# Attention and GeGLU block: runs of five overlapping tokens on even and odd partitions, another load order on two queues, and batches 1 and 2 prepared inside blocks 0 and 1

## Chip, cores and metric

One core of one Trainium2 chip runs the whole program. The metric is the device time of one execution in microseconds (us), smaller is better. The kernel before was timed in 3 runs; the median stands for it.

## What is computed

The inputs are q, k and v (8 batches, 8 heads, 576 tokens, 64 features, float32) and three weights. Attention without a token-by-token matrix comes first, then a gated feed-forward over all 4608 tokens:

```python
q_s = softmax(q, axis=-1)            # over the 64 features
k_s = softmax(k, axis=2)             # over the 576 tokens
kv  = einsum('bhsd,bhse->bhde', k_s, v)
att = einsum('bhsd,bhde->bhse', q_s, kv)
x   = att.transpose(0, 2, 1, 3).reshape(4608, 512)
out = (gelu(x @ w_gate) * (x @ w_val)) @ w_out      # 512 -> 1536 -> 512
```

## The kernel before

The order of the work on every engine is the order of the program text: nothing is rescheduled. Eight batches are eight blocks of 512 tokens; the last 64 tokens of each batch (its remainder) are gathered in `xtr`, and all eight remainders make a ninth block of 512 tokens.

**Attention of a batch** has these steps. `exp_main` and `exp_rem` (L127 to L139) turn q and k into `eq` and `ek` on ACT, by Exp. `cast_v_main` and `cast_v_rem` copy v to float16 on POOL. `norm_sum` and `norm_mul` (L156 to L171) divide `eq` by its sums per token and head on DVE, four heads at a time. `unit_kv` (L175) multiplies `ek` and v for two pairs of heads on PE (10 matmuls) and scales the product into `kv_sb` on DVE. `unit_t` (L198) transposes `eq` on PE and copies it to `eqt` on DVE; `unit_trem` does it for the remainder. `unit_x` (L223) multiplies `kv_sb` and `eqt` into `psx`, and a copy puts it in `xt`, the input of the block; `unit_xrem` fills `xtr`.

**A block** is twelve steps `ffn_fi` (L241): four matmuls into `psg` and four into `psv`, then Gelu on ACT (`gl`) and a product on DVE (`ht`). Below, FI 3 is the fourth of these steps. `ffn_out` (L259) then takes four slices of 128 tokens (NS 0 to 3), 12 matmuls each, into `psy`; DVE copies each to `yo`, and stores go out. `psg`, `psv` and `psy` share six PSUM buffers, the pieces of attention two others.

**Order.** All loads are on the queue of SP: k, v, q of batch 0 in two halves of heads, then weights, then batch 1. A DMA for 512 tokens puts four consecutive tokens on each of 128 partitions (packets of 1 KB); a second one puts the 64 tokens of the remainder on 64 partitions (packets of 256 B). Attention of batch 0 stands ahead of block 0. That of batch 1 stands behind the twelve steps of block 0, between and after its slices NS 1 to 3, and likewise batch 2 in block 1. From block 2 on, the attention of the next batch rides inside the twelve steps (`attention_units`, `norm_units`), and the Exp of the batch after that stands behind them.

Of the kernel before, what the change touches and what calls it, by code (L numbers as in the profile page):

```python
# [18 lines left out]
def kernel(  # L19
# [392 lines left out]
```

## Time and profile before

| | us |
|---|---|
| median of 3 runs | 353.28 (353.16 to 353.89) |
| profiled execution | 353.71 |
| its span, first to last instruction | 351.8 |
| PE busy | 319.6 (91%) |
| DVE, ACT, POOL busy | 179.9, 135.7, 42.4 |
| mean DMA rate | 135 GB/s |

A profile row names the line, the engine, the operation, the tile written and the tiles read, and the shape. Matmul rows overlap, so a busy PE is not a PE at its peak rate; what counts is when a matmul follows which.

### The profile page before, as it was taken

Reading aid. Unit: us, or ns where it says so; the run is one execution under the profiler, and the core shown is the slowest. Engines: PE = TensorE matmul, PEld = TensorE weight load, DVE = VectorE, ACT = ScalarE, POOL = GpSimd, SP = SyncE. Lnnn points to the kernel's source line nnn. Section 1 sums busy time; section 2 is a strip of 40 time slices with the busy share of each in tenths; the row PEclk is TensorE's granted clock in tenths of the full one; section 3 lists DMA queues with packets and bytes.
Section 4 is the critical chain, followed back from the end, with each engine's and each line's share of the span. In section 5 each row is a group of like instructions: output and inputs, shape, how many; then the busy total and the mean of one; then the engine's idle time right before and its main releaser. Section 6 shows DMA issues by size and latency. Waiting matters only on the chain.

```text
span 351.8 us, 4287 instructions
## 1 busy us (share of the span) xinstructions
PE 319.6 (91%) x1680; PEld 152.8 (43%) x1680; DVE 179.9 (51%) x283; ACT 135.7 (39%) x184; POOL 42.4 (12%) x36
## 2 busy tenths in 40 slices
PE   0259999499987999999999999999999999999994
PEld 0234445244443544454444444544544444444441
DVE  2582337934386963396339524953494334334331
ACT  3403363043762247424743483248325123203310
POOL 2376620402000200002000200020000000000000
PEclk9999999789996999999999999999999999999999
DMA  7999999893016900296039404940300020011013
GB/s 192 330 388 386 344 278 284 241 269 94 3 60 188 270 6 2 96 276 153 0 117 287 120 2 135 277 112 0 121 1 0 8 113 0 2 60 60 2 30 89
DMA packets 45395, 47.45 MB, mean 135 GB/s; under 512 B 13632, under 2 KB 38208, under 8 KB 45376
## 3 DMA queue, kind: packets, MB, share of 16 engines
q1 hardware_dynamic: 45376, 47.19, 46.3%
q8 instruction: 13, 0.21, 0.3%
q14 instruction: 6, 0.05, 0.1%
HBM read 37.75 MB, written 9.44 MB: 134 GB/s over the span
## 4 chain that ended last, share of the span: by engine, by line
PE 85%; DVE 10%; DMA 2%; issue 1%; SPq 1%; ACT 0%
PE psg L244 27%; PE psv L248 27%; PE psy L262 24%; DVE eq L169 3%; DVE rq L159 2%; PE psx L226 2%; DMA qt<-in_q_dram 2%; PE pst L205 2%; PE pskv L180 2%; DVE xt L229 1%; DVE yo L267 1%; DVE eqt L208 1%; DVE kv_sb L188 1%; PE pstr L214 1%; DVE rrq L163 0%
## 5 line engine op out<-in xcount | busy, mean ns | idle before, releaser
L253 DVE SCALAR_TENSOR_TENSOR ht<-psv,gl 128x512 f16<-128x512 f32 x108 | 74.1, 686 | 92.1 <-PE psv L248 91.5
L251 ACT ACTIVATE gl<-psg 128x512 f32<-128x512 f32 x108 | 64.5, 597 | 144.7 <-PE psg L244 136.1
L244 PE MATMUL psg<-xt,wg_sb 128*128 128x512 f16 x384 | 101.8, 389 | 0.0
L248 PE MATMUL psv<-xt,wv_sb 128*128 128x512 f16 x384 | 99.5, 382 | 0.0
L262 PE MATMUL psy<-wo_sb,ht 128*128 128x512 f16 x432 | 95.0, 379 | 0.0
L248 PEld LDWEIGHTS <-wv_sb 128*128 128x128 f16 x432 | 42.6, 99 | 52.5 <-issue 2.7
L262 PEld LDWEIGHTS <-ht 128*128 128x128 f16 x432 | 41.8, 98 | 49.4
L244 PEld LDWEIGHTS <-wg_sb 128*128 128x128 f16 x432 | 41.6, 99 | 46.0 <-issue 2.8
L267 DVE TENSOR_SCALAR yo<-psy 128x512 f32<-128x512 f32 x36 | 24.8, 690 | 60.7 <-PE psy L262 60.7
L147 POOL CAST v<-vt 128x2048 f16<-128x2048 f32 (+1 forms) x9 | 16.4, 1824 | 179.7 <-DMA vt<-in_v_dram 166.6
L159 DVE TENSOR_REDUCE rq<-eq 128x20 f32<-128x1280 f16 x16 | 23.6, 1476 | 9.6 <-ACT eq L136 9.6
L169 DVE TENSOR_TENSOR eq<-eq,rrq 128x1280 f16<-128x1280 f16 x16 | 25.4, 1590 | 0.2
L205 PE MATMUL pst<-ident,eq 128*128 128x128 f16 x128 | 11.5, 242 | 14.5 <-DVE rck L185 7.8
L180 PE MATMUL pskv<-v,ek 128*128 128x130 f16 x160 | 12.6, 231 | 9.9 <-POOL v L147 9.5
L129 ACT ACTIVATE eq<-qt 128x2048 f16<-128x2048 f32 (+1 forms) x9 | 15.4, 1709 | 6.4 <-DMA qt<-in_q_dram 6.4
L205 PEld LDWEIGHTS <-eq 128*128 128x128 f16 x128 | 9.0, 108 | 19.3 <-DVE eq L169 9.3
L180 PEld LDWEIGHTS <-ek 128*128 128x128 f16 x160 | 11.1, 102 | 13.7 <-ACT ek L129 6.0
L129 ACT ACTIVATE ek<-kt 128x2048 f16<-128x2048 f32 (+1 forms) x9 | 15.5, 1719 | 3.6 <-DMA kt<-in_k_dram 3.5
L238 ACT CAST xtr<-psxr 128x256 f16<-128x256 f32 x8 | 3.0, 372 | 34.9 <-PE psxr L236 34.9
L226 PE MATMUL psx<-eqt,kv_sb 128*128 128x512 f16 x32 | 14.0, 463 | 1.9 <-DVE eqt L208 1.1
L231 ACT CAST xt<-psx 128x512 f16<-128x512 f32 x20 | 11.7, 585 | 9.6 <-PE psx L226 9.6
L248 PE MATMUL psv<-xtr,wv_sb 128*128 128x512 f16 x48 | 12.3, 379 | 0.0
(33 smaller groups left out, 121.1 us busy)
## 6 DMA issues: line engine op xcount, KB each, us to landing
out_dram<-yo SPq DMA_DIRECT2D x16, 512.0 KB, 2.6
kt<-in_k_dram SPq DMA_DIRECT2D x7, 1024.0 KB, 7.9
vt<-in_v_dram SPq DMA_DIRECT2D x7, 1024.0 KB, 10.3
qt<-in_q_dram SPq DMA_DIRECT2D x7, 1024.0 KB, 10.3
wgst<-in_moe_w_gate_dram SPq DMA_DIRECT2D x3, 1024.0 KB, 12.3
wvst<-in_moe_w_val_dram SPq DMA_DIRECT2D x3, 1024.0 KB, 13.6
wost<-in_moe_w_out_dram SPq DMA_DIRECT2D x3, 1024.0 KB, 14.6
kt<-in_k_dram SPq DMA_DIRECT2D x2, 512.0 KB, 5.9
```

The source lines that it names most:

```text
L129: nc.scalar.activation(out=dst[:, 0:NM, h0 * D:h1 * D].rearrange("p n (h d) -> p h n d", d=D), in_=tiles[(nm, b)][:, h0:h1, :].rearrange(" ...
L159: nc.vector.reduce_sum(rq, eq_b[b % 2][:, :, h0 * D:h1 * D].rearrange("p n (h d) -> p n h d", d=D), axis=mybir.AxisListType.X)
L169: nc.vector.tensor_tensor(out=e, in0=e, in1=rr[(b, h0)].unsqueeze(-1).to_broadcast((P, NM + 1, n, D)), op=ALU.mult)
L180: nc.tensor.matmul(pskv[:, j, :], ek_b[b % 2][:, n, hp * P:(hp + 1) * P], v16_b[b % 2][:, n, 2 * hp:2 * hp + 2, 0:VW], start=(n == 0), sto ...
L205: nc.tensor.transpose(pst[:, j, n * P:(n + 1) * P], eq_b[b % 2][:, n, hp * P:(hp + 1) * P], ident)
L226: nc.tensor.matmul(psx, st[(b, "kv", hp)].rearrange("p h e -> p (h e)"), st[(b, "eqt")][:, hp, 0:MAIN], start=True, stop=True)
L244: nc.tensor.matmul(psg, wg_sb[:, ci, fi * P:(fi + 1) * P], xt[:, ci, :], start=(ci == 0), stop=(ci == HP - 1))
L248: nc.tensor.matmul(psv, wv_sb[:, ci, fi * P:(fi + 1) * P], xt[:, ci, :], start=(ci == 0), stop=(ci == HP - 1))
L251: nc.scalar.activation(out=gl, in_=psg, func=ACTF.Gelu)
L253: nc.vector.scalar_tensor_tensor(out=ht, in0=psv, scalar=_H_SCALE, in1=gl, op0=ALU.mult, op1=ALU.mult)
L262: nc.tensor.matmul(psy, hts[fi][:, ns * P:(ns + 1) * P], wo_sb[:, fi, :], start=(fi == 0), stop=(fi == NFI - 1))
L267: nc.vector.tensor_scalar(out=yo[:, ns % 2, :], in0=psy, scalar1=1.0 / _H_SCALE, scalar2=None, op0=ALU.mult)
```

## The change

A batch is now seen as 64 runs of nine tokens. Run m lies on partitions 2m and 2m+1: the even one holds its tokens 0 to 4, the odd one its tokens 4 to 8, so token 4 is loaded twice. Position 0 counts on even partitions alone: v there is multiplied by `even` (1 on even partitions, 0 on odd ones), and the column of ones with it. The remainder of a batch is now the first token of each run, position 0, and the separate loads, Exps and casts of remainders are gone. Each load becomes two DMAs, one for the even and one for the odd partitions. For batch 0 one goes to SP's queue and one to ACT's, in the order q, k, v, with position 0 of q left for later (`q0r`, `eq0r`). Weights come in halves of the former pieces, through eight buffers of their own. Before and during batch 0, 22 matmuls whose product nobody reads are issued (`warm_pe`), and tables of ACT are loaded by an Exp and a Gelu on a tile `tiny` (`preload`). The first three steps of block 1 are split by head pairs (`ffn_first`), block 0 takes `psy` in two halves of six matmuls (NS 0 to 3 the first halves, NS 4 to 7 the second), the ninth block stands before the last batch, and the last stores go out on two queues.

```diff
-    def load_main(src, nm, b, h0, h1):
+    def load(src, nm, b, h0, h1, n0, engs):
         key = (nm, b)
         if key not in tiles:
-            tiles[key] = ldp.tile([P, H, NM * D], f32, name=f"{nm}t", tag="ld")
+            tiles[key] = ldp.tile([P, H, NC * D], f32, name=f"{nm}t", tag="ld")
+        for t in range(2):
+            engs[t].dma_start(
+                out=tiles[key][t:P:2, h0:h1, n0 * D:NC * D],
+                in_=src[b, h0:h1].rearrange("h (m n) d -> m h (n d)", n=NT)[
+                    :, :, (4 * t + n0) * D:(4 * t + NC) * D])
...
-    def load_rem(src, nm, b):
-        t = rmp.tile([64, H, D], f32, name=f"{nm}r", tag="rm")
-        nc.sync.dma_start(out=t, in_=src[b, :, MAIN:S, :].rearrange("h p d -> p h d"))
-        tiles[(nm + "r", b)] = t
-    def load_batch(b):
-        for src, nm in ((k, "k"), (v, "v"), (q, "q")):
-            load_main(src, nm, b, 0, H)
-            load_rem(src, nm, b)
...
+    def cast_v(b, h0, h1, eng="pool", parts=(0, 1)):
+        t, d = tiles[("v", b)], v16_b[b % 2]
+        if 1 in parts:
+            copy_on(eng, d[:, 1:NC, h0:h1, 0:D].rearrange("p n h d -> p h n d"),
+                    t[:, h0:h1, D:NC * D].rearrange("p h (n d) -> p h n d", d=D))
+        if 0 in parts:
+            dst, src = d[:, 0, h0:h1, 0:D], t[:, h0:h1, 0:D]
+            if eng == "act":
+                nc.scalar.activation(out=dst, in_=src, func=ACTF.Copy, scale=even[:, 0:1])
+            else:
+                (nc.gpsimd if eng == "pool" else nc.vector).tensor_scalar(
+                    out=dst, in0=src, scalar1=even[:, 0:1], scalar2=None, op0=ALU.mult)
+    def norm(b, hp, eng="dve", n0=0, n1=NC):
+        n = n1 - n0
+        e = eq_b[b % 2][:, n0:n1, hp * P:(hp + 1) * P].rearrange("p n (h d) -> p n h d", d=D)
+        rq = att.tile([P, n, 2], f32, name="rq", tag="rq", bufs=4)
+        nc.vector.reduce_sum(rq, e, axis=mybir.AxisListType.X)
+        rrq = att.tile([P, n, 2], f32, name="rrq", tag="rrq", bufs=4)
         nc.vector.reciprocal(out=rrq, in_=rq)
-        rr[(b, h0)] = rrq
-    def norm_mul(b, h0, h1):
-        n = h1 - h0
-        e = eq_b[b % 2][:, :, h0 * D:h1 * D].rearrange("p n (h d) -> p n h d", d=D)
+        (nc.gpsimd if eng == "pool" else nc.vector).tensor_tensor(
+            out=e, in0=e, in1=rrq.unsqueeze(-1).to_broadcast((P, n, 2, D)), op=ALU.mult)
...
+    def warm_pe(n):
+        ps = ps_big.tile([P, 512], f32, name="pswarm", tag="mm")
+        for _ in range(n):
+            nc.tensor.matmul(ps, ident, warm, start=True, stop=True)
+    def preload(func):
+        nc.scalar.activation(out=tiny, in_=tiny, func=func)
...
+    def ffn_first(xt, after):
+        ps = []
+        for fi in range(len(after)):
+            psg = ps_big.tile([P, 512], f32, name="psg", tag="mm")
+            mm_gv(psg, wg_sb, xt, fi, range(0, 2))
+            psv = ps_big.tile([P, 512], f32, name="psv", tag="mm")
+            mm_gv(psv, wv_sb, xt, fi, range(0, 2))
+            ps.append((psg, psv))
+            for f in after[fi]:
+                f()
+        for fi, (psg, psv) in enumerate(ps):
+            mm_gv(psg, wg_sb, xt, fi, [2])
+            mm_gv(psv, wv_sb, xt, fi, [2])
+        hts = []
+        for fi, (psg, psv) in enumerate(ps):
+            mm_gv(psg, wg_sb, xt, fi, [3])
+            mm_gv(psv, wv_sb, xt, fi, [3])
+            hts.append(gate(psg, psv))
+        return hts
...
+    QA = (nc.sync, nc.scalar)
+    load(q, "q", 0, 0, 4, 1, QA)
+    load(q, "q", 0, 4, 8, 1, QA)
+    load(k, "k", 0, 0, H, 0, QA)
+    load(v, "v", 0, 0, H, 0, QA)
+    for c in range(NW):
         load_w_gv(c)
     for c in range(3):
         load_w_o(c)
+    load(q, "q", 1, 0, H, 0, SY2)
+    for c in range(3, NO):
+        load_w_o(c)
+    for h0 in (0, 4):
+        load(k, "k", 1, h0, h0 + 4, 0, SY2)
+        load(v, "v", 1, h0, h0 + 4, 0, SY2)
+    nc.sync.dma_start(out=q0r, in_=q[0].rearrange("h (m n) d -> m h (n d)", n=NT)[:, :, 0:D])
...
+    preload(ACTF.Exp)
+    exp("q", 0, 0, 4, 1)
+    exp("q", 0, 4, 8, 1)
+    exp("k", 0, 0, 4)
+    exp("k", 0, 4, 8)
+    preload(ACTF.Gelu)
+    warm_pe(16)
+    norm(0, 0, "dve", 1)
+    norm(0, 1, "pool", 1)
+    norm(0, 2, "dve", 1)
+    norm(0, 3, "pool", 1)
+    unit_t(0, 0, "dve")
+    warm_pe(6)
+    cast_v(0, 0, 4, "dve")
+    cast_v(0, 4, 6, "act")
+    cast_v(0, 6, 8, "pool")
+    unit_t(0, 1, "dve")
...
+    cast_w("wg", 0, "pool", 0, 128)
+    unit_x(0, 0, "act", True)
...
+    at(0, FI, NFI - 1, L(exp, "q", 1), L(exp, "k", 1, 0, 4),
+       L(cast_w_o, 3), L(cast_w_o, 4, "dve"), L(norm, 1, 0), L(cast_w_o, 5),
+       L(norm, 1, 1, "pool"), L(norm, 1, 2), L(cast_v, 1, 0, 4),
+       L(norm, 1, 3, "pool"), L(exp, "k", 1, 4, 8), L(cast_v, 1, 4, 6, "act"), L(cast_v, 1, 6, 8),
+       L(preload, ACTF.Gelu))
+    at(0, NS, 5, L(unit_t, 1, 0))
+    at(0, NS, 6, L(unit_kv, 1, 0))
+    at(0, NS, 7, L(unit_x, 1, 0, "act", True), L(unit_x, 1, 1, "dve", True),
+       L(unit_t, 1, 1))
+    first1 = [[L(unit_kv, 1, 1)], [L(unit_x, 1, 2, "act")], [L(unit_x, 1, 3, "dve")]]
...
+    at(1, FI, 4, L(norm, 2, 1))
+    at(1, FI, 5, L(norm, 2, 2))
+    at(1, FI, 6, L(norm, 2, 3))
+    at(1, FI, 7, L(unit_t, 2, 0))
+    at(1, FI, 8, L(exp, "k", 2), L(cast_v, 2, 0, H))
+    at(1, FI, 9, L(unit_t, 2, 1))
+    at(1, FI, 10, L(unit_trem, 2))
+    at(1, FI, 11, L(unit_kv, 2, 0), L(unit_kv, 2, 1), L(load_batch, 3),
+       L(exp, "q", 3), L(exp, "k", 3), L(exp_rem0), L(cast_v, 3, 0, H))
+    at(1, NS, 0, L(unit_x, 2, 0, "dve"), L(unit_x, 2, 1, "dve"))
+    at(1, NS, 1, L(unit_x, 2, 2, "dve"), L(unit_x, 2, 3, "dve"))
+    at(1, NS, 2, L(unit_xrem, 2, "dve"))
+    at(1, NS, 3, L(norm_rem0))
+    at(2, FI, 5, L(unit_trem, 0))
+    at(2, FI, 8, L(unit_xrem, 0))
...
+            for i in range(HP):
+                at(b, FI, i, L(norm, n, i))
+            at(b, FI, 0, L(unit_kv, n, 0))
+            at(b, FI, 2, L(unit_kv, n, 1))
+            at(b, FI, 4, L(unit_t, n, 0))
+            at(b, FI, 6, L(unit_t, n, 1))
+            at(b, FI, 7, L(unit_trem, n))
+            for i in range(HP):
+                at(b, FI, 7 + i, L(unit_x, n, i))
+            at(b, FI, 11, L(unit_xrem, n))
```

The loads at the start, on SP's queue (`kt`, `vt`, `qt` are the tiles of 512 tokens or, now, of five positions; `kr`, `vr`, `qr` the remainders; `wgst` and `wvst` weights before their cast). Before:

```order
L89 DMA kt<-in_k_dram 128x4x256
L95 DMA kr<-in_k_dram 64x8x64
L89 DMA vt<-in_v_dram 128x4x256
L95 DMA vr<-in_v_dram 64x8x64
L89 DMA qt<-in_q_dram 128x4x256
L95 DMA qr<-in_q_dram 64x8x64
L89 DMA kt<-in_k_dram 128x4x256
L89 DMA vt<-in_v_dram 128x4x256
L89 DMA qt<-in_q_dram 128x4x256
L109 DMA wgst<-in_moe_w_gate_dram 128x4x512
```

Now, on the same queue (ACT's queue has the first three rows as well, for the odd partitions):

```order
L104 DMA qt<-in_q_dram 64x4x256 x2
L104 DMA kt<-in_k_dram 64x8x320
L104 DMA vt<-in_v_dram 64x8x320
L115 DMA wgst<-in_moe_w_gate_dram 128x4x256
L115 DMA wvst<-in_moe_w_val_dram 128x4x256
```

q moved from third to first, remainders are gone, and each row fills 64 partitions.

DVE between the last `ht` of block 0 and the first `xt` of batch 1 (`rq` and `rrq` are the sums and their reciprocals, `rck` belongs to `kv_sb`). Before:

```order
L253 SCALAR_TENSOR_TENSOR ht<-psv,gl 128x512 x12
L267 TENSOR_SCALAR yo<-psy 128x512 x2
L185 RECIPROCAL rck<-pskv 128x2
L188 SCALAR_TENSOR_TENSOR kv_sb<-pskv,rck,mask 128x128 x2
...
L159 TENSOR_REDUCE rq<-eq_104 128x20
L163 RECIPROCAL rrq<-rq 128x20
L169 TENSOR_TENSOR eq_104<-eq_104,rrq 128x5x256
L267 TENSOR_SCALAR yo<-psy 128x512
```

Now:

```order
L272 SCALAR_TENSOR_TENSOR ht<-psv,gl 128x512 x12
L125 CAST wo_sb<-wost 128x1024
L165 TENSOR_REDUCE rq<-eq_108 128x10
L167 RECIPROCAL rrq<-rq 128x10
L168 TENSOR_TENSOR eq_108<-eq_108,rrq 128x5x128
...
L340 TENSOR_SCALAR yo<-psy 128x512 x2
L125 COPY eqt<-pst 128x2x512
L340 TENSOR_SCALAR yo<-psy 128x512
L196 RECIPROCAL rck<-pskv 128x2
L199 SCALAR_TENSOR_TENSOR kv_sb<-pskv,rck,mask 128x128 x2
```

All four sums (one per pair of heads) and two of the four products now stand ahead of the first `yo`; the other two products went to POOL.

ACT in block 1, where `gl` is the Gelu. Before:

```order
L251 ACTIVATE gl<-psg 128x512 x12
L129 ACT_TABLE_LOAD
L129 ACTIVATE ek_96<-kt 128x8x4x64
L136 ACTIVATE ek_96<-kr 64x512
L129 ACTIVATE eq_97<-qt 128x8x4x64
L136 ACTIVATE eq_97<-qr 64x512
```

Now:

```order
L270 ACTIVATE gl<-psg 128x512 x4
L143 ACT_TABLE_LOAD
L143 ACTIVATE eq_103<-qt 128x8x5x64
L270 ACT_TABLE_LOAD
L270 ACTIVATE gl<-psg 128x512
L123 CAST xtr<-psxr 128x4x64
...
L143 ACT_TABLE_LOAD
L143 ACTIVATE ek_102<-kt 128x8x5x64
L270 ACT_TABLE_LOAD
```

The two Exps of batch 2 moved from behind the twelve Gelus to places after the fourth and the ninth, each between two table loads.

## Rows read from the trace of the kernel before

**Rows 1.** The page: its head, and PE's busy tenths in 40 slices.

```profile
span 351.8 us, 4287 instructions
...
PE   0259999499987999999999999999999999999994
```

**Rows 2.** Windows: stretch, length, busy us (instructions) of PE, PEld, DVE, ACT, POOL, clock, DMA share, GB/s.

```profile
60.00:80.00 20.00, 15.04 (x75) 6.94 (x73) 13.31 (x17) 4.56 (x7) 4.17 (x3) 0.83 0.97 256
```

**Rows 3.** The chain that ended last: start us, length us, what.

```profile
26.69 1.71 PE psg L244 x4
...
30.11 1.56 PE psg L244 x4
...
35.98 0.86 PE psg L244 x4
...
136.72 10.36 PE psy L262 x48
...
171.18 10.36 PE psy L262 x48
...
336.72 10.37 PE psy L262 x48
```

**Rows 4.** Timeline of the start: start us, length us, engine, line, operation, [idle before <-releaser].

```profile
4.90 1.06 ACT L129 ACTIVATE ek<-kt 128x1024 f16<-128x1024 f32 x1 [2.89 <-DMA kt<-in_k_dram]
...
6.58 0.63 ACT L136 ACTIVATE ek<-kr 64x512 f16<-64x512 f32 x1 [0.62 <-DMA kr<-in_k_dram]
...
13.21 1.06 ACT L129 ACTIVATE ek<-kt 128x1024 f16<-128x1024 f32 x1 [0.63 <-DMA kt<-in_k_dram]
...
16.19 1.06 ACT L129 ACTIVATE eq<-qt 128x1024 f16<-128x1024 f32 x1 [1.93 <-DMA qt<-in_q_dram]
...
19.34 1.24 PE L180 MATMUL pskv<-v,ek 128*128 128x130 f16 x10 [0.45 <-DVE xt L229]
...
26.50 1.90 PE L244 MATMUL psg<-xt,wg_sb 128*128 128x512 f16 x4
```

**Rows 5.** Timeline between blocks 0 and 1.

```profile
62.68 1.89 POOL L147 CAST v<-vt 128x2048 f16<-128x2048 f32 x1 [10.56 <-DMA vt<-in_v_dram]
62.72 3.20 DVE L169 TENSOR_TENSOR eq<-eq,rrq 128x1280 f16<-128x1280 f16 x1
64.52 1.87 POOL L152 CAST v<-vr 64x512 f16<-64x512 f32 x1
...
70.70 1.84 PE L244 MATMUL psg<-xt,wg_sb 128*128 128x512 f16 x4
```

**Rows 6.** Timeline in block 1 and at the start of block 2.

```profile
97.41 1.31 PE L180 MATMUL pskv<-v,ek 128*128 128x130 f16 x20
...
111.60 1.87 PE L244 MATMUL psg<-xt,wg_sb 128*128 128x512 f16 x4
```

**Rows 7.** Lines, shapes apart: engine, operation, count | busy us, mean ns | idle before.

```profile
L169 DVE TENSOR_TENSOR eq<-eq,rrq 128x1280 f16<-128x1280 f16 x16 | 25.4, 1590 | 0.2
L159 DVE TENSOR_REDUCE rq<-eq 128x20 f32<-128x1280 f16 x16 | 23.6, 1476 | 9.6 <-ACT eq L136 9.6
L129 ACT ACTIVATE eq<-qt 128x2048 f16<-128x2048 f32 x7 | 13.3, 1895 | 0.6 <-DMA qt<-in_q_dram 0.6
L208 DVE COPY eqt<-pst 128x1024 f16<-128x1024 f16 x16 | 10.8, 682 | 0.9 <-PE pst L205 0.9
L188 DVE SCALAR_TENSOR_TENSOR kv_sb<-pskv,rck,mask 128x128 f16<-128x128 f32 x32 | 9.7, 346 | 0.6
L129 ACT ACT_TABLE_LOAD x7 | 9.0, 1283 | 0.8 <-PEq L396 0.7
L163 DVE RECIPROCAL rrq<-rq 128x20 f32<-128x20 f32 x16 | 4.4, 278 | 0.6
```

**Rows 8.** Timeline of the end: the last instruction on an engine other than SP.

```profile
347.11 0.69 DVE L267 TENSOR_SCALAR yo<-psy 128x512 f32<-128x512 f32 x1 [1.90 <-PE psy L262]
```

**Rows 9.** Windows, a stretch in which only weights are loaded (columns as in rows 2).

```profile
18.00:20.00 2.00, 1.55 (x9) 0.70 (x8) 1.50 (x3) 0.00 (x0) 1.05 (x1) 1.00 1.05 386
```

More of the change, by code (lines that the diff above doesn't have):

```diff
@@ L178, in unit_kv @@
             hp = 2 * g + j
-            for n in range(NM + 1):
+            for n in range(NC):
                 nc.tensor.matmul(
@@ new lines, in evac, with store @@
+        rows = out[b * S:(b + 1) * S, :].rearrange("(m n) c -> m n c", n=NT)
+        def store(eng, t, n0, n1, c0, c1):
+            eng.dma_start(out=rows[:, 4 * t + 1 + n0:4 * t + 1 + n1, c0:c1],
+                          in_=yo_t[b][t:P:2, n0 % 2:n0 % 2 + n1 - n0, c0:c1])
+        if b == order[-1] and ns == 3:
+            hc = C // 2
+            nc.vector.tensor_scalar(out=yo[:, 0:hc], in0=psy[:, 0:hc], scalar1=1.0 / _H_SCALE,
+                                    scalar2=None, op0=ALU.mult)
+            nc.scalar.activation(out=yo[:, hc:C], in_=psy[:, hc:C], func=ACTF.Copy,
+                                 scale=1.0 / _H_SCALE)
+            store(nc.sync, 0, ns, ns + 1, 0, C)
+            store(nc.scalar, 1, ns, ns + 1, 0, C)
+            return
@@ new lines, in evac @@
+        nc.vector.tensor_scalar(out=yo, in0=psy, scalar1=1.0 / _H_SCALE,
+                                scalar2=None, op0=ALU.mult)
+        if b == order[-1]:
+            store(nc.sync, 0, ns, ns + 1, 0, C)
+            store(nc.scalar, 1, ns, ns + 1, 0, C)
+        elif ns % 2 == 1:
+            for t in range(2):
+                store(nc.sync, t, ns - 1, ns + 1, 0, C)
+    QA = (nc.sync, nc.scalar)
+    load(q, "q", 0, 0, 4, 1, QA)
+    load(q, "q", 0, 4, 8, 1, QA)
+    load(k, "k", 0, 0, H, 0, QA)
@@ L330, with load_batch @@
-    unit_x(0, 3)
-    unit_xrem(0)
-    for c in range(3):
-        cast_w_gv(c)
+    load(q, "q", 1, 0, H, 0, SY2)
[5 more added lines that the diff above has]
+    nc.sync.dma_start(out=q0r, in_=q[0].rearrange("h (m n) d -> m h (n d)", n=NT)[:, :, 0:D])
+    def load_batch(b):
+        for src, nm in ((q, "q"), (k, "k"), (v, "v")):
+            load(src, nm, b, 0, H, 0, SY2)
+    load_batch(2)
@@ L353, with ride @@
+    def ride(b, kind, i):
+        for fn in plan.get((b, kind, i), []):
+            fn()
+    for b in order:
+        xt = get_xt(b) if b < B else xtr
+        hts = []
+        fi0 = 0
+        if b == 1:
+            hts = ffn_first(xt, first1)
+            fi0 = 3
+            ride(b, FI, 2)
+        for fi in range(fi0, NFI):
             hts.append(ffn_fi(xt, fi))
-            if fi < len(norms):
-                norms[fi]()
-            if units[fi] is not None:
-                units[fi]()
+            ride(b, FI, fi)
@@ new lines @@
+            for ns in range(4):
+                psys.append(ps_big.tile([P, C], f32, name="psy", tag="mm"))
+                mm_out(psys[ns], hts, ns, range(0, NFI // 2))
+                ride(b, NS, ns)
+            for ns in range(4):
+                mm_out(psys[ns], hts, ns, range(NFI // 2, NFI))
+                evac(b, ns, psys[ns])
+                ride(b, NS, 4 + ns)
+        else:
+            for ns in range(4):
+                psy = ps_big.tile([P, C], f32, name="psy", tag="mm")
+                mm_out(psy, hts, ns, range(NFI))
+                evac(b, ns, psy)
+                ride(b, NS, ns)
```

294 lines of the change are left out of this document (123 added, 171 removed).

## Prediction, made before the change was run

> **What bounds the kernel now.** I read the page first. Its head gives a span of 351.8 us, and PE's row of tenths shows 9 in nearly all slices, with three weak places: the first three slices (8.8 us each), slice 8 and slice 12 [rows 1]. So PE is the bound, except at the start and at two handovers. The windows confirm it for the first handover: from 60 to 80 us PE is busy 15.04 of 20 us at a granted clock of 0.83, while DVE has 13.31 us of work [rows 2].
>
> The chain of waits then gives the undisturbed pace. Four matmuls take 0.86 us, and the output stages of two neighbouring blocks start 171.18 - 136.72 = **34.46 us** apart [rows 3]. A block is 144 matmuls of 512 columns, 144 x 0.86 / 4 = 31.0 us, so attention of one batch costs PE about 3.4 us.
>
> The timelines give the starts of the blocks: the first `psg` of block 0 at 26.50 [rows 4], of block 1 at 70.70 [rows 5], of block 2 at 111.60 [rows 6]. That splits the span into a start of 26.5, block 0 with 44.2, block 1 with 40.9, and 240.2 for the rest. Against 34.46, block 0 loses 9.7 and block 1 loses 6.4. Of the 9.7, some 2.4 are clock: the first three groups of four matmuls take 1.71, 1.71 and 1.56 us instead of 0.86 (the first and the last of the three stand in [rows 3]); 0.43 us for one matmul is the lower level, 1.2 GHz, and PE had worked only in pieces before. The other 7.3 are the handover. Block 2 starts slowly as well: 136.72 - 111.60 = 25.1 us to its output stage, where block 3 takes 171.18 - 136.72 - 10.36 = 24.1, so 1.0 is lost there.
>
> So there are three places to gain: 26.5 us of start, 9.7 and 6.4. The change touches all three. The rest stays, since PE's work per block stays.
>
> **The start.** In the kernel before, the first load, 0.52 MB, has landed when Exp starts at 4.90. The second halves of v and q, 0.52 MB each, land between 13.21 and 16.19: 1.05 MB in 2.98 us, 352 GB/s with packets of 1 KB [rows 4]. Now q comes first. Its first half (0.52 MB) lands at 4.9 and its second at 6.4; k and v are 1.31 MB each in packets of 1.25 KB, 3.7 us each at that rate, so k lands at 10.1 and v at 13.8. Two queues bring no rate: one queue already moves 386 GB/s where only weights are loaded [rows 9].
>
> Exp and the normalising of q (some 6 us of DVE and ACT) fit between 4.9 and 13.8, and Exp of k ends near 12.7, so v is late last. Behind v: the cast of four heads on one engine (2048 elements take 1.89 us [rows 5], so 1.0, and 0.3 for position 0), to 15.1; 20 `pskv` matmuls, at 1.24 us for ten as in the start before [rows 4], to 17.6; four `psx` matmuls at 0.43, each one behind its `kv_sb` (0.35 [rows 7]), to **19.3**. First weights (0.52 MB each) land at 15.3 and 16.8, and their quarter casts are over by 20. Gain: 26.5 - 19.3 = 7.2.
>
> The clock at block 0's start could cost nothing, or 2.4 as before. The 22 added matmuls lie too early to settle it (they end before v is there), but PE works nearly without a break from 15.1 on. I take the middle, **1.2**.
>
> **Block 0 to block 1.** With 20.7 us for twelve steps, the last Gelu ends near 41.0. By then the queue has brought 6.29 MB of weights (31.7 at 352 GB/s), half of w_out (1.57 MB, 35.7) and q of batch 1 (39.4). The rest of w_out lands at 43.5, needed at 46.5, when the first halves of `psy` end. k and v of batch 1 come in halves at 45.3, 47.2, 49.0 and 50.9. So ACT, not DMA, releases q: table load 1.28, then 2560 elements at 1895 ns for 2048 [rows 7], 2.37: done at 44.7.
>
> DVE then has four sums (640 elements each, half of 1476 ns), four reciprocals (0.2 each) and two products (half of 1590 ns) [rows 7]: 5.4 us. A product can also have to wait for POOL. In [rows 5] a product took 3.20 us instead of 1.59 while POOL cast v from 62.68, and POOL's next small cast 1.87 us. I add one such turn, 0.8, and DVE is done at 50.9. Two `yo` (0.69 [rows 8]) end at 52.3, the `eqt` copy (0.68) at 53.0, one more `yo` and two `kv_sb` with their reciprocal at 54.5. PE reaches the end of the output stage at 52.9 and then waits for these, with 1.3 us of its own work between: 1.7 us lost, 0.7 in the split steps, and 0.4 for the clock. I take **2.8** where 7.3 stood. POOL's product has no row: between the cast rate (0.6 us) and twice DVE's time (1.6) it ends by 49.0, when PE first needs it.
>
> The Trainium skill says of this pair of engines (SBUF — State Buffer, Who interferes with whom) that a DVE instruction with two SBUF inputs and a GpSimd instruction that reads SBUF exclude each other for the whole instruction. The trace agrees (3.20 against 1.59). It speaks against moving products to POOL beside DVE: with a turn for both of DVE's products the sum would be 0.8 higher, with none 0.8 lower.
>
> **Block 1.** Now it holds Exp of q and k of batch 2, each between two table loads: 2 x 1.28 + 2.37 = 4.9 us in which no Gelu runs. Nothing hidden would cost 9.9, all hidden 0. Six PSUM buffers let PE run three steps ahead, 5.2 us, so the first Exp alone just fits. But DVE gets a sum, a reciprocal and a product (1.7) beside each `ht` (0.69) in four steps: 2.4 us a step where PE needs 1.73. Stepping through, with psg of FI 3 done at 0: Exp ends at 4.4, DVE has pairs 0 and 1 at 8.8 where PE wants to transpose them at 8.1, and pairs 2 and 3 at 13.8 where PE comes at 12.8; one `psv` waits 0.2. Together **2.0**, near the lower end. What was behind block 1 (6.4) goes, since `psx` of batch 2 now lies between the output slices.
>
> **The rest.** From block 2 on the work per block is the same in other positions: sums in four pieces instead of two (6.9 us of DVE a block instead of 6.7) and Exp of 2560 elements instead of two pieces, on engines with room. Loads grow by a ninth, stores are cut in two; both are hidden, at 34 us a block. The remainder of batch 0 now rides in block 2: 8 of 48 attention matmuls, 0.4 of its 3.4 us. Block 2's slow start (1.0) goes, as PE comes from a full stage. The last `yo` is halved over two engines: -0.3. Rest: 240.2 - 1.0 + 0.4 - 0.3 = 239.3.
>
> **Sum.** 19.3 + (34.5 + 1.2 + 2.8) + (34.5 + 2.0) + 239.3 = 333.6 us of span. The profiled execution took 353.71 for its span of 351.8, 1.9 more, and lies 0.4 above the median 353.28. So 333.6 + 1.9 - 0.4 = **335 us** beside 353.3, 5% less.
>
> **Rivals.**
> 1. *Nothing comes late*, 329 us. The clock is up at block 0's start (-1.2) and for `pskv` (20 in 1.31 [rows 6] instead of 2.5: -1.2), the handover costs only PE's order (0.8, so -2.0), and block 1 does not stall (-2.0). For it: six buffers are deep. Against it: DVE's 2.4 us a step.
> 2. *The handover and block 1 stay late*, 342 us. POOL and DVE take turns more often, the handover costs 7.3 as before (+4.5), and block 1 stalls one whole Exp with its loads (4.9, so +2.9). For it: POOL has six instructions there, all reading SBUF.
> 3. *Slower than before*: loads that fill only every second partition run at half the rate, 176 GB/s. Then v lands at 24.3 and block 0 starts 10.5 later; behind the weights, q, k and v of batch 1 take 22 us instead of 11, the last of v lands at 72.6, and its product on PE moves from 56.8 to 74. With another 1.5 for v of batch 2 the time is 354. It is above the median where the rate is under some 178 GB/s. For it: the only kind of load on 64 partitions before, as `kr`, takes 1.68 us for 0.13 MB, 78 GB/s [rows 4]. Against it: `kr` is 512 packets, and 512 packets of 1 KB take 1.5 us too, so the packets explain it.
> 4. *The extra matmuls and the second queue do nothing*: that is in the sum already, up to the 1.2 of clock.
>
> To rival 3: the Trainium skill (SBUF — State Buffer, Door 1: The DMA port swizzle) gives 196 GB/s for partitions 0 to 63 against 328 for all; at that ratio, an estimate, the time would be 345. Its own table puts even and odd partitions in every port, so by that table even ones alone lose nothing. No row here shows such a load.
>
> **Chances.** The forecast (331 to 340) 0.64, rival 1 with all below it 0.14, rival 2 with what lies up to 350 0.17, rival 3 0.05. The range reaches from rival 1 to just above rival 2, 329 to 343, and leaves out under 2 in 10. A measurement of this kernel tells 0.2%, 0.7 us, from no change. Faster: 0.95, all but rival 3. Of its 0.05, 0.01 falls within 0.2% and 0.04 above.
>
> **What would show it.** First `psg` of block 0 near 19.3; `qt`, `kt`, `vt` landing near 6.4, 10.1, 13.8; 39 us between the first matmuls of blocks 0 and 1, 36.5 from block 1 to 2, 34.5 from then on. In the waits, `psx` or `psg` behind DVE at the handover, and `pst` behind DVE's product in block 1. Wrong would be a v that lands after 17, `psg` waiting for a weight cast, or blocks of more than 35 from block 2 on, which would mean that DVE or ACT has become the bound.

## The result and the profile after

| | before | predicted | after |
|---|---|---|---|
| median, us | 353.22 (353.09 to 353.89, 4 runs) | 335.0 (329 to 343) | **335.14** (334.31 to 336.04, 4 runs) |
| ratio after/before, 95% interval | | 0.948 | 0.9485 (0.9458 to 0.9513) |
| start, to the first `psg` of block 0 | 26.5 | 19.3 | 19.7 |
| block 0, first `psg` to first `psg` | 44.2 | 38.5 | 35.0 |
| block 1 | 40.9 | 36.5 | 38.2 |
| from block 2 to the end | 240.2 | 239.3 | 240.6 |
| span of the profiled execution | 351.8 | 333.6 | 333.5 |

Two executions among the experiments below, one of the kernel before (494 us) and the profiled one of the kernel without the unread matmuls (483 us), ran at a mean granted clock of 0.67; no median or reading below uses them.

The total came out as forecast, and the start and the two handovers all shrank. The sizes did not come out as forecast: block 0 took 3.5 us less than the sum says, and all other terms took more. The page of the changed kernel (compare [rows 1]; PEclk is the granted clock in tenths):

```profile
span 333.5 us, 4470 instructions
...
PE   8499998998999999999999999999999999999994
...
PEclk9879999999999999999999999999999999999998
...
PE 62%; DVE 20%; issue 6%; ACT 5%; DMA 4%; POOL 1%; SPq 0%; DVEq 0%; ACTq 0%; POOLq 0%
```

The holes at the handovers are gone from PE's row: between the second and the last no slice is under 8, where 4 and 7 stood before. The start as a timeline (start us, length us, engine, line, operation, [idle before <-releaser]), to be read beside [rows 4]:

```profile
12.17 2.43 ACT L143 ACTIVATE ek<-kt 128x1280 f16<-128x1280 f32 x2 [4.73 <-DMA kt<-in_k_dram]
...
14.11 0.69 DVE L125 CAST v<-vt 128x1024 f16<-128x1024 f32 x1 [2.42 <-DMA vt<-in_v_dram]
...
14.62 1.28 ACT L260 ACT_TABLE_LOAD   x1
...
15.56 1.24 PE L191 MATMUL pskv<-v,ek 128*128 128x130 f16 x10 [2.79 <-DVE v L158]
...
16.02 0.61 ACT L123 CAST v<-vt 128x512 f16<-128x512 f32 x1
...
16.98 1.24 PE L191 MATMUL pskv<-v,ek 128*128 128x130 f16 x10 [0.17 <-ACT v L156]
...
19.72 1.61 PE L265 MATMUL psg<-xt,wg_sb 128*128 128x512 f16 x4
```

v lands at 14.1, but k only at 12.2: SP's half of k is still moving while ACT's half of v moves. So Exp of k ends at 14.6, the table load for Gelu stands behind it, ACT's part of v behind that, and the second ten `pskv` wait for ACT, though only 0.17 us. In seven traces whose start is this same program, the first cast of v begins between 14.1 and 15.4 us and the first `psg` between 18.8 and 20.7. A difference of under 2 us at the start of one trace therefore says little by itself. The windows of the same stretch and of one in block 2 (stretch, length, busy us of PE, PEld, DVE, ACT, POOL, granted clock, DMA share, GB/s):

```profile
4.00:6.00 2.00, 2.00 (x6) 0.63 (x5) 0.00 (x0) 1.99 (x3) 0.00 (x0) 1.00 1.03 344
...
8.00:10.00 2.00, 0.44 (x8) 0.27 (x7) 1.90 (x5) 0.00 (x0) 1.04 (x1) 1.00 1.00 327
10.00:12.00 2.00, 1.72 (x14) 0.84 (x11) 1.65 (x4) 0.00 (x0) 0.72 (x1) 1.00 1.06 391
...
18.00:20.00 2.00, 2.00 (x8) 0.68 (x6) 1.51 (x5) 1.05 (x2) 1.53 (x2) 0.50 1.09 385
...
99.00:101.00 2.00, 2.00 (x16) 1.05 (x14) 1.93 (x5) 0.60 (x1) 0.00 (x0) 1.00 1.03 360
...
105.00:107.00 2.00, 1.97 (x13) 0.86 (x11) 1.93 (x4) 0.60 (x1) 0.00 (x0) 1.00 1.07 395
```

Loads that fill every second partition run at 327 to 395 GB/s here (the 385 at 18 to 20 us are weights), so rival 3 (176 GB/s) is out. The clock is at its lower level, 1.2 GHz, at 18 to 20 us. The handover between blocks 0 and 1, beside [rows 5]:

```profile
42.27 2.34 ACT L143 ACTIVATE eq<-qt 128x2560 f16<-128x2560 f32 x1
...
47.77 1.26 POOL L168 TENSOR_TENSOR eq<-eq,rrq 128x640 f16<-128x640 f16 x1 [4.29 <-DVE rrq L167]
...
48.97 1.70 POOL L121 CAST v<-vt 128x1024 f16<-128x1024 f32 x1
...
50.61 0.22 DVE L167 RECIPROCAL rrq<-rq 128x10 f32<-128x10 f32 x1
...
51.63 0.73 PE L191 MATMUL pskv<-v,ek 128*128 128x130 f16 x10 [0.85 <-POOL v L158]
...
53.68 0.65 PE L243 MATMUL psx<-eqt,kv_sb 128*128 128x512 f16 x2
54.75 0.76 PE L265 MATMUL psg<-xt,wg_sb 128*128 128x512 f16 x2
```

Exp of q is done at 42.27 + 2.34 = 44.6 (forecast 44.7), DVE's last reciprocal at 50.8 (forecast 50.9). PE's waits here sum to about 1.7 us. The longest, 0.85, is not behind DVE but behind POOL's part of v: its cast began 0.02 us behind a product of DVE (48.95, 0.83 us) and took 1.70, where a cast of this size took 1.04 at 39.62. In block 1 `pst` waits for DVE's products, as forecast, and in block 2 it waits again, there for DVE's copy `eqt`:

```profile
70.34 0.83 DVE L168 TENSOR_TENSOR eq<-eq,rrq 128x640 f16<-128x640 f16 x1
...
71.23 0.40 PE L216 MATMUL pst<-ident,eq 128*128 128x128 f16 x4 [0.53 <-DVE eq L168]
...
76.17 0.40 PE L216 MATMUL pst<-ident,eq 128*128 128x128 f16 x4 [0.87 <-DVE eq L168]
...
92.90 1.03 PE L265 MATMUL psg<-xt,wg_sb 128*128 128x512 f16 x4
93.71 0.68 DVE L178 TENSOR_REDUCE rq<-eq0r 128x8 f32<-128x512 f16 x1
94.65 0.69 DVE L181 TENSOR_TENSOR eq0r<-eq0r,rrq 128x512 f16<-128x512 f16 x1
...
107.79 0.61 PE L216 MATMUL pst<-ident,eq 128*128 128x128 f16 x8 [0.82 <-DVE eqt L125]
```

The chain gives block 2's length: from 92.90 to its output stage 25.45 us, where block 3 takes 152.92 - 118.35 - 10.36 = 24.21 (beside [rows 3]). From there on blocks follow each other by 34.56.

```profile
19.93 1.41 PE psg L265 x4
...
118.35 10.36 PE psy L309 x48
...
152.92 10.36 PE psy L309 x48
...
187.48 10.36 PE psy L309 x48
```

### The profile page after: what moved, and what is told of

Its sections match the earlier page's. It is cut to its first block, busy times and chain, and to the rows that moved or that the text cites. A ratio compares the mean times of both kernels' runs of the same rounds, so it can differ in the third digit from the quotient of the medians.

```text
span 333.5 us, 4470 instructions
## 1 busy us (share of the span) xinstructions
PE 319.0 (96%) x1702; PEld 153.0 (46%) x1702; DVE 181.4 (54%) x330; ACT 143.5 (43%) x186; POOL 50.3 (15%) x50
## 4 chain that ended last, share of the span: by engine, by line
PE 62%; DVE 20%; issue 6%; ACT 5%; DMA 4%; POOL 1%; SPq 0%; DVEq 0%; ACTq 0%; POOLq 0%
PE psy L309 24%; PE psg L265 17%; PE psv L265 16%; DVE ht L272 7%; DVE rq L165 5%; DMA kt<-in_k_dram 3%; DVE eq L168 3%; PE psx L243 3%; DVE rrq L167 2%; ACT ek L143 1%; DVE eqt L125 1%; DVE kv_sb L199 1%; ACT L143 1%; PE pskv L191 1%; ACT eq L143 1%
## 5 line engine op out<-in xcount | busy, mean ns | idle before, releaser
L265 PE MATMUL psg<-xt,wg_sb 128*128 128x512 f16 x384 | 100.3, 381 | 0.1
L340 DVE TENSOR_SCALAR yo<-psy 128x512 f32<-128x512 f32 x31 | 21.3, 689 | 49.1 <-PE psy L309 49.1
L121 POOL CAST v<-vt 128x2048 f16<-128x2048 f32 (+2 forms) x9 | 15.0, 1670 | 144.2 <-DMA vt<-in_v_dram 103.0
L165 DVE TENSOR_REDUCE rq<-eq 128x10 f32<-128x640 f16 (+1 forms) x32 | 25.4, 793 | 8.5 <-ACT eq L143 8.3
L168 DVE TENSOR_TENSOR eq<-eq,rrq 128x640 f16<-128x640 f16 (+1 forms) x28 | 23.1, 823 | 1.0
L123 ACT CAST xt<-psx 128x512 f16<-128x512 f32 x24 | 14.1, 586 | 18.3 <-PE psx L243 18.3
L143 ACT ACTIVATE ek<-kt 128x2560 f16<-128x2560 f32 (+1 forms) x10 | 18.9, 1898 | 6.2 <-DMA kt<-in_k_dram 6.2
L143 ACT ACTIVATE eq<-qt 128x2560 f16<-128x2560 f32 (+1 forms) x9 | 18.5, 2052 | 0.4 <-DMA qt<-in_q_dram 0.3
L191 PE MATMUL pskv<-v,ek 128*128 128x130 f16 x160 | 12.8, 231 | 3.9 <-DVE v L158 2.8
L243 PE MATMUL psx<-eqt,kv_sb 128*128 128x512 f16 x32 | 12.1, 411 | 0.3
L265 PE MATMUL psg<-xtr,wg_sb 128*128 128x512 f16 x48 | 12.3, 379 | 0.0
```

Source lines behind the costliest of these rows:

```text
L121: nc.gpsimd.tensor_copy(out=dst, in_=src)
L143: nc.scalar.activation(out=dst[:, n0:NC, h0 * D:h1 * D].rearrange("p n (h d) -> p h n d", d=D), in_=tiles[(nm, b)][:, h0:h1, n0 * D:NC * D ...
L165: nc.vector.reduce_sum(rq, e, axis=mybir.AxisListType.X)
L168: (nc.gpsimd if eng == "pool" else nc.vector).tensor_tensor(out=e, in0=e, in1=rrq.unsqueeze(-1).to_broadcast((P, n, 2, D)), op=ALU.mult)
L191: nc.tensor.matmul(pskv[:, j, :], ek_b[b % 2][:, n, hp * P:(hp + 1) * P], v16_b[b % 2][:, n, 2 * hp:2 * hp + 2, 0:VW], start=(n == 0), sto ...
L243: nc.tensor.matmul(psx, st[(b, "kv", hp)].rearrange("p h e -> p (h e)"), st[(b, "eqt")][:, hp, 0:MAIN], start=True, stop=True)
```

## The experiments

They were timed in three sets on three chips, each beside the kernel before, whose median lay between 352.1 and 353.5 us. The unaltered change was timed again only in the last set (335.47). Differences are to its first result, 335.14, unless said otherwise, so those of under 1 us are shown only where two kernels stand in the same set or a trace shows the place.

**The load order of batch 0.** k, v, q instead of q, k, v, and Exp of k before Exp of q:

```diff
-    load(q, "q", 0, 0, 4, 1, QA)
-    load(q, "q", 0, 4, 8, 1, QA)
     load(k, "k", 0, 0, H, 0, QA)
     load(v, "v", 0, 0, H, 0, QA)
+    load(q, "q", 0, 0, 4, 1, QA)
+    load(q, "q", 0, 4, 8, 1, QA)
```

> The changed kernel with one part undone: batch 0 loads k, v, q instead of q, k, v (same pieces, same two queues), and ACT takes Exp of k before Exp of q. Theory (q first hides Exp, sums, products and transposes of q behind the loads of k and v): q's second half now lands near 14, the products end 5 us after its Exp, near 20, the transposes and pskv follow in PE's order, first psg near 25 instead of 19.7, total near 340 (+5). Rival (the last load sets the start whatever it is, since the bytes are the same): first psg within 0.7 of 19.7, total 335.

Measured 339.03, ratio 0.9617 (0.9579 to 0.9655): +3.9.

```profile
12.13 1.06 ACT L143 ACTIVATE eq<-qt 128x1024 f16<-128x1024 f32 x1 [2.22 <-DMA qt<-in_q_dram]
...
23.96 1.34 PE L265 MATMUL psg<-xt,wg_sb 128*128 128x512 f16 x4
```

Exp of q starts at 12.13, its last product ends at 19.5, and the first `psg` is at 23.96. So the order is worth 4 us: q has the longest chain behind it (sums, products, transposes). Even in the old order the first `psg` comes 2.5 us ahead of the 26.50 of the kernel before; no run parts what of this is the layout without remainders, what the casts of v on three engines, and what the tables loaded ahead.

**One queue.**

```diff
-    QA = (nc.sync, nc.scalar)
+    QA = (nc.sync, nc.sync)
```

> The changed kernel with the loads of batch 0 for odd partitions on SP's queue too, none on ACT's. Theory (two queues bring no rate; served at uneven speed they let the two halves of k land at 10.0 and 12.1): k has landed by 10.5, v by 14, first psg between 19.2 and 19.8, total 334.6 to 335.3. Rival (the second queue saves issue time that counts at the start): v lands after 15, first psg after 20.7, total over 336.

Measured 336.32, ratio 0.9531 (0.9478 to 0.9583): +1.2, but this interval overlaps that of the change, and the time alone is not clear of noise. The first cast of v begins at 15.99 and the first `psg` at 21.27, later than in any of the seven traces of the same start. The windows of this run:

```profile
4.00:6.00 2.00, 2.00 (x9) 0.77 (x8) 0.00 (x0) 0.53 (x1) 0.00 (x0) 1.00 0.85 247
...
8.00:10.00 2.00, 0.38 (x4) 0.24 (x4) 1.90 (x6) 0.30 (x1) 0.80 (x1) 1.00 0.94 282
```

247 and 282 GB/s stand where two queues moved 344 and 327. In the ten traces with this order on two queues, these windows moved 304 to 377 and 327 to 383 GB/s; from 6 to 8 us there is no difference (281 against 282 to 371). The theory falls, and with it the prediction's sentence on queues, on one trace with one queue. Issue time alone does not explain it: SP had issued k by 4.8 us, and it landed by 12.67. The Trainium skill says that more issuing queues bring no bandwidth and only save issue time (DMA: Bandwidth & Descriptors, Rules for kernel authors); for these loads the measurement differs. Why one queue reaches 360 to 395 GB/s with loads of the same kind at 99 to 107 us stays open. The order has a part in it: with k and v first, two queues moved 385 to 395 GB/s from 4 to 10 us.

**The matmuls nobody reads.** Once left out, and once kept, with twelve more just ahead of the key-value matmuls:

```diff
-    warm_pe(16)
...
-    warm_pe(6)
```

> The changed kernel without its 22 matmuls whose product nobody reads. Theory (they end before v lands, and the granted clock is 0.5 again from 14 to 20 us): first psg within 0.3 of 19.7 and its first group of four within 0.3 of 1.4 us, total 335 to 335.5. Rival (they buy the early end of the low clock in block 0): the first groups take 1.7, 1.7 and 1.6 us as in the kernel before, total 336.3.

Measured 335.08, ratio 0.9509 (0.9462 to 0.9556): no difference in the total. Where its first `psg` starts and how long its first group takes, the other half of the expectation, is not shown.

```diff
     unit_t(0, 1, "dve")
+    warm_pe(12)
     unit_kv(0, 0)
```

> The changed kernel with 12 more matmuls whose product nobody reads, on PE between the second transposes of batch 0 and the first pskv, where PE sat idle from 12.8 to 15.6. Theory (the clock is what makes pskv, psx and the first psg slow there): granted clock 1.00 from 14 to 22, ten pskv in 0.7 instead of 1.24, no slow group at the start of block 0, together 1.4 us less, total 333.7. Rival (casts on ACT and DVE set the start, the clock lies beside them): first psg within 0.3 of 19.7, total 335 less at most 0.6 for the first group.

Measured 334.45, ratio 0.9491 (0.9454 to 0.9529): -0.7, and 0.6 less than the run without the 22, which stands in the same set. The ten `pskv` take 0.73 us instead of 1.24, and the clock stays at 2.4 GHz:

```profile
15.82 0.73 PE L191 MATMUL pskv<-v,ek 128*128 128x130 f16 x10 [0.53 <-DVE v L158]
...
18.59 1.34 PE L265 MATMUL psg<-xt,wg_sb 128*128 128x512 f16 x4
```

The 22 matmuls of the change end at 11.5 us. From the last transpose, at 12.8, to the first `pskv` PE stands, and the granted clock is 0.52 from 14 to 16 us. Twelve placed in that gap bring half of what I expected. From the first cast of v to the first `psg` it takes 4.23 us, where the seven traces without them take 4.55 to 5.61. Block 1 starts 1.4 us earlier than in the change (53.34 against 54.75), but 0.6 of it is lost there, and 0.8 is left at block 2's start (92.10 against 92.90):

```profile
73.07 1.89 POOL L121 CAST v<-vt 128x2048 f16<-128x2048 f32 x1 [9.28 <-DMA vt<-in_v_dram]
...
73.88 1.76 DVE L168 TENSOR_TENSOR eq<-eq,rrq 128x640 f16<-128x640 f16 x1
```

POOL's cast of batch 2's v begins between 73.0 and 73.4 us in the change, in this run and in four others, though block 1 starts at 53.1 to 54.8; here it waits for its load. The earlier block brings DVE's last product of batch 2 into it: 1.76 us instead of 0.83, and PE waits 1.80 for it instead of 0.87.

**Products of block 1 on POOL.**

```diff
-    at(1, FI, 4, L(norm, 2, 1))
+    at(1, FI, 4, L(norm, 2, 1, "pool"))
...
-    at(1, FI, 6, L(norm, 2, 3))
+    at(1, FI, 6, L(norm, 2, 3, "pool"))
```

> Two of batch 2's four products in block 1 go from VectorE to GpSimd. Theory: block 1 takes 38.15 us from its first gate matmul to block 2's, about 2.4 more than its matmuls need, and transposes wait 0.53 and 0.87 us there for VectorE's products (0.83 us each); GpSimd's product of the same size took 1.26 us in block 0. With two of the four on GpSimd VectorE has 1.7 us less to do, block 1 shrinks by 1.2 to 1.4 us, and the total is 333.8 us. Rival: GpSimd's 1.26 us and its turns with VectorE give the wait back, and the total stays at 335.1.

Measured 336.36, ratio 0.9511 (0.9465 to 0.9556): no gain. In the trace 1.0 us is a later start (first `psg` at 20.70, v's cast at 15.4), which the edit does not touch. Block 1 took 94.53 - 55.80 = 38.7 us, 0.6 more, as the rival said:

```profile
71.55 1.26 POOL L168 TENSOR_TENSOR eq<-eq,rrq 128x640 f16<-128x640 f16 x1 [16.55 <-PE psv L265]
...
72.86 0.40 PE L216 MATMUL pst<-ident,eq 128*128 128x128 f16 x4 [1.10 <-POOL eq L168]
```

**The remainder of batch 0 later.**

```diff
-    at(1, NS, 3, L(norm_rem0))
-    at(2, FI, 5, L(unit_trem, 0))
-    at(2, FI, 8, L(unit_xrem, 0))
+    at(4, NS, 3, L(norm_rem0))
+    at(6, NS, 0, L(unit_trem, 0))
+    at(6, NS, 1, L(unit_xrem, 0))
```

> The remainder of batch 0 (sums, product, transposes, its one matmul group) moves from blocks 1 and 2 to blocks 4 to 6. Theory: its 1.6 us of VectorE at 93.7 us stand ahead of the first activation products of block 2, and its buffers hold up the transposes at 107.8 (0.82 us); block 2 took about 1.1 us more than later blocks, and about 0.8 of that goes: 334.3 us. Rival: the same work stalls a later block as much, and the total stays at 335.1.

Measured 334.22, ratio 0.9455 (0.9416 to 0.9493): -0.9. Block 2 starts at 92.95 and reaches its output stage at 117.33, after 24.38 us instead of 25.45:

```profile
117.33 10.36 PE psy L309 x48
```

Of the 1.1 us, 0.8 is the wait for `eqt` at 107.79, which is gone, and some 0.3 the remainder's own eight matmuls, which now stand in block 6. Most of it comes back in the profile: block 5's output stage follows block 4's by 34.93 instead of 34.57, with a wait of 0.4 for `eqt`, and the eight matmuls are paid in block 6. At the next output stage 0.3 is left (287.38 against 287.70). This profile is of the slowest of the four executions (334.95), and the interval overlaps that of the change; so this run alone does not tell whether 0.3 or 0.9 is gained.

**Batch 2 behind block 1 again.** Exp, products, transposes, key-value and `psx` matmuls of batch 2 go behind block 1's twelve steps, to NS 1 to 3 (two lines of the edit):

```diff
-    at(1, FI, 3, L(exp, "q", 2), L(norm, 2, 0))
...
+    at(1, NS, 1, L(unit_kv, 2, 0), L(unit_kv, 2, 1), L(norm, 2, 0), L(norm, 2, 1))
```

> Batch 2's attention is put behind block 1's gate and up matmuls again, as all later batches stand. Theory: as part of block 1 it cost 2.4 us of stall, behind the slices it costs the slow start of block 2 that the kernel before showed (about 6.5 us in all, some of it clock): block 1 and the start of block 2 together take 4.1 us more, about 339 us. Rival: the first blocks' waits are the loads' and batch 0's, so that the place of batch 2 costs nothing, and the total stays at 335.1.

Measured 341.40, ratio 0.9653 (0.9611 to 0.9694): +6.3.

```profile
90.49 0.40 PE L216 MATMUL pst<-ident,eq 128*128 128x128 f16 x4 [1.61 <-DVE eq L168]
...
92.40 0.61 PE L216 MATMUL pst<-ident,eq 128*128 128x128 f16 x4 [1.51 <-DVE eq L168]
```

Block 1 took 43.3 us (53.83 to 97.1) instead of 38.15, since `pst` waits 1.61 and 1.51 us for DVE's products behind the output slices. Then block 2 starts at 1.2 GHz (1.71 us for four `psg`) and takes 37.0 instead of 35.65. The direction was right; block 1 (+5.1) and block 2 (+1.4) together came out 2.4 dearer than the 4.1 I had expected.

**Batch 1 behind block 0 again**, once with the key-value matmuls first as before, once with q first:

```diff
...
+    at(0, NS, 1, L(unit_kv, 1, 0), L(unit_kv, 1, 1), L(norm, 1, 0), L(norm, 1, 1))
+    at(0, NS, 2, L(norm, 1, 2), L(norm, 1, 3))
...
```

Both edits also undo what belongs to the place: the halves of `psy` in block 0, the split first steps of block 1, the products on POOL and the cast of v shared with ACT.

> Batch 1's attention is put behind block 0's gate and up matmuls again, with block 0's output sums no longer split in halves of w_out; batch 2 stays inside block 1. Theory: this was the dearest stretch of the kernel before, where the tensor engine stood for about 8 us in all between blocks 0 and 1 against 1.7 now: 341 us, 5 to 8 more than the change as it stands. Rival: the order within block 0 matters little because the loads of batch 1 set its pace, and the total is within 1.5 us of 335.1.

Measured 350.18, ratio 0.9911 (0.988 to 0.9942): +15, where I expected 5 to 8.

```profile
49.15 1.90 POOL L121 CAST v<-vt 128x2048 f16<-128x2048 f32 x1 [6.43 <-DMA vt<-in_v_dram]
...
52.63 2.32 PE L191 MATMUL pskv<-v,ek 128*128 128x130 f16 x20 [6.68 <-POOL v L158]
```

The loads of the change bring v of batch 1 last. With the key-value matmuls first PE stood 6.68 us for v, of which some 3.5 are its cast, whole on POOL here, and the products, in DVE's queue behind `kv_sb`, stood as well. This mixes place and order, so the second run puts q first (against the run before):

```diff
-    at(0, NS, 1, L(unit_kv, 1, 0), L(unit_kv, 1, 1), L(norm, 1, 0), L(norm, 1, 1))
-    at(0, NS, 2, L(norm, 1, 2), L(norm, 1, 3))
+    at(0, NS, 0, L(norm, 1, 0), L(norm, 1, 1))
+    at(0, NS, 1, L(norm, 1, 2), L(norm, 1, 3))
+    at(0, NS, 2, L(unit_t, 1, 0))
...
```

> Batch 1's attention behind block 0's gate and up matmuls as in the run of 350 us, but in the order in which its loads arrive: products and transposes of q first, then the key-value matmuls. Theory: of that run's 15 us the most is order, not place: the tensor engine stood 6.7 us for v and the products were queued behind the key-value sums on VectorE. With q first block 1 starts at about 57.8 us instead of 69.2 (54.8 in the change as it stands), the total is about 339 us. Rival: the place decides, and the total stays at 347 or more.

Measured 340.75, ratio 0.9668 (0.9612 to 0.9724): +5.6. So 9.4 of the 15 us are order, and 5.6 are the place with what was undone beside it.

```profile
62.27 1.89 PE L265 MATMUL psg<-xt,wg_sb 128*128 128x512 f16 x4
```

The clock takes part: it is at 0.50 from 56 to 66 us. Block 1 starts at 62.27, not at the 57.8 I expected; the trace is of an execution of 343.12 us, 2.4 above the median.

**Together, and the change once more.** The late warm-up matmuls and the late remainder in one kernel; the same with the table load behind ACT's cast of v; and the change unaltered beside them.

> The late warm-up matmuls and the late remainder of batch 0 together. Theory: they act in different places (the start, block 2), so their gains add: 0.8 and 0.9 us, 333.4 us. Rival: the remainder's work in blocks 4 to 6 gives its part back, and only the warm-up's 0.8 is left: 334.3 us.

> The run before, and ScalarE's table load for Gelu is put behind its cast of batch 0's v. Theory: in the changed kernel the second ten key-value matmuls wait for that cast, which stands behind the table load (1.28 us) though v has landed; the cast starts 1.3 us earlier, the second ten 0.5 us earlier, and the total falls by about 0.5 us to 332.9 us. Rival: v lands when k's exponentials end, and VectorE's and GpSimd's parts of v end as late as ScalarE's: no gain, 333.4 us.

```diff
-    preload(ACTF.Gelu)
     warm_pe(16)
...
     cast_v(0, 4, 6, "act")
+    preload(ACTF.Gelu)
```

> The changed kernel as it stands, beside the others. Theory: 335.1 us; its first gate matmul starts between 18.8 and 20.7 us, as it did in runs whose start is the same program.

| | median, us (6 runs) | ratio, interval | first cast of v | first `psg` | between |
|---|---|---|---|---|---|
| change once more | 335.47 (334.77 to 335.92) | 0.9501 (0.9459 to 0.9543) | 15.14 | 19.73 | 4.59 |
| both | **333.90** (333.46 to 334.45) | 0.9459 (0.9418 to 0.9501) | 15.56 | 19.61 | 4.05 |
| both, table load later | 334.11 (333.96 to 336.43) | 0.9476 (0.9427 to 0.9525) | 14.28 | 18.33 | 4.05 |

By the medians the gains add: 335.47 - 333.90 = 1.6 us, and no run of the one reaches the other's. This version beats both kernels. Moving the table load brings no gain in the total. In both runs 4.05 us lie between v's first cast and `psg`, but in the second v came so late (15.56) that the table load no longer stood in its way. With v at 14.36, and the table load still ahead of the cast, the run with the late warm-up matmuls took 4.23: so it costs 0.2 there, not the 0.5 expected. When v lands moves from run to run (14.1 to 15.6), and it moves the start with it.

The third kernel has two runs of 336.0 and 336.4 among four of 334; its profile is of 336.01. Its block 1 took 94.06 - 53.08 = 41.0 us instead of 38.15. Its timeline there, and its windows:

```profile
73.35 1.89 POOL L121 CAST v<-vt 128x2048 f16<-128x2048 f32 x1 [9.25 <-DMA vt<-in_v_dram]
...
73.62 2.29 DVE L168 TENSOR_TENSOR eq<-eq,rrq 128x640 f16<-128x640 f16 x1
...
75.98 0.40 PE L216 MATMUL pst<-ident,eq 128*128 128x128 f16 x4 [2.34 <-DVE eq L168]
```

```profile
74.00:76.00 2.00, 0.02 (x1) 0.03 (x2) 2.00 (x2) 1.98 (x2) 2.00 (x2) 1.00 0.00 0
...
78.00:80.00 2.00, 2.00 (x9) 1.00 (x8) 1.92 (x4) 0.00 (x0) 0.00 (x0) 0.50 0.00 0
```

POOL's cast began 0.27 us before DVE's product, and the product took 2.29 us instead of 0.83. PE stood 2.34 us for it, and the clock then fell to 0.50. So a start 1.4 us earlier than the change's became a block 2 that starts 1.2 later (94.06 against 92.90). Whether the other long run is such a case is not shown. In the change's own profile the product began first, took 0.83, and POOL's cast took 2.12 instead of 1.89:

```profile
72.78 0.83 DVE L168 TENSOR_TENSOR eq<-eq,rrq 128x640 f16<-128x640 f16 x1
...
73.24 2.12 POOL L121 CAST v<-vt 128x2048 f16<-128x2048 f32 x1 [9.95 <-ACT gl L270]
```

The Trainium skill has this rule (SBUF — State Buffer, Who interferes with whom): the order of issue decides which of the two stands. The trace agrees, in both orders.

## Why the prediction was right, and where it was not

- **The total** is right within 0.2 us, 335.14 against 335.0. The mechanism was right too: the change shortens the start and two handovers, and four undo runs put prices on them: order of the loads 3.9, second queue 1.2 (not clear of noise), batch 1 inside block 0 5.6, batch 2 inside block 1 6.3. That is 17.0 of the 18.1 us gained. They need not add up exactly, and the third holds what was undone beside the place. The layout itself was not undone in any run.
- **The agreement to 0.2 us is luck.** Against the sum, -3.5 in block 0 stands beside +0.4 in the start, +1.7 in block 1 and +1.3 in the rest: errors of both signs that cancel.
- **The start**, 19.3 against 19.7. In the profiled execution q (6.4) and v (13.8 against 14.1) landed as forecast; in others q's second half came up to 2.3 us later and v up to 1.5. "k lands at 10.1" was wrong: only ACT's half did (9.97), SP's half landed at 12.1, while v of the other queue was moving beside it. I had treated the loads as if they came one by one; that this is the cause is not shown, since on one queue k came no earlier (12.67).
- **"Two queues bring no rate"** was wrong: on one queue these loads ran at 247 to 332 GB/s between 4 and 12 us, on two at 327 to 391 in the change. I had taken the 386 of [rows 9], a stretch of weights, for a rule on all loads. The forecast for two queues used 352 GB/s and was near.
- **The clock at block 0's start**, 1.2 in the sum. The first four `psg` took 1.41 us in the chain instead of 0.86, so about 0.6. That the 22 matmuls do not settle it was right: without them the total is the same, and with twelve in the right place the clock stays up.
- **The handover**, 2.8 in the sum, 1.7 measured. The two times it rests on (44.7, 50.9) were right to 0.1, the second by chance: no product of DVE waited for POOL, so the 0.8 added for that did not come, but sums, reciprocals and gaps took as much more. The turn fell on POOL's cast of v instead, and PE's longest wait was behind POOL, not behind DVE. The landing times ahead of it mix 352 and 386 GB/s for weights; the last v was there at 49.6, not 50.9. Block 0 was shorter by 3.5 altogether. Beside the 0.6 of clock and the 1.1 of the handover, some 1.4 us of batch 1's matmuls (ten `pskv`, two `psx`, the remainder's) stand behind its end, in block 1, where I had counted whole blocks; 0.4 stays open.
- **Block 1**, 2.0 in the sum, 2.4 measured beside what its matmuls need, at the place named: `pst` behind DVE's product (0.53 and 0.87). What a product on POOL would cost was put between 0.6 and 1.6; it is 1.26, too slow to help here.
- **The rest**, 1.3 more than the sum: 0.9 in block 2, and 0.1 in each of the four blocks behind it (34.56 against 34.46). "Block 2's slow start (1.0) goes" was wrong. The clock's part went, but the remainder of batch 0, which I had costed as 0.4 us of PE, put a sum, a reciprocal and a product (1.6 us) on DVE ahead of block 2's own, and `pst` then waited 0.8 for `eqt`.
- A slip in reading [rows 1]: the second weak slice, the 7, is the thirteenth, not slice 12.

## What to carry to other kernels

Load first what has the longest chain behind it (3.9 us here), and order the work by arrival: 9.4 us hung on that order in one place, against 5.6 on where the work stood. Matmuls for the clock paid here only next to the work they were for (0.6 to 0.7 us); 22 that ended 4 us earlier changed nothing. Work that costs PE little is still to be counted on the engine that carries it. A product of DVE that PE waits for should not share its time with a cast on POOL, and a gain at the start can move the one into the other: here the cast's time did not follow the start, the product's did.

## What was not expected of the hardware

A second queue went with a higher rate of the first loads: 344 against 247 GB/s (4 to 6 us) and 327 against 282 (8 to 10 us), though one queue reaches 395 later; the cause is open. And DVE and POOL take turns by who starts first. A cast begun 0.27 us ahead made one product 2.29 us long instead of 0.83, one begun 0.81 ahead 1.76. In the first case, with PE's wait of 2.34 and the lower clock behind it, block 1 took 2.8 us more; in the second, in which the clock stayed at 1.00, 0.6.
